# The merges of the triangular inverses: two heads in turn product by product, and the first group's second half in slot 1

## The chip, the cores and the metric

One core of a Trainium2 chip runs the whole program. The metric is the time of one execution on the device in microseconds; the time given for a kernel is the median of its runs. A profile is one further execution, recorded by the hardware profiler: its span runs from the first to the last instruction.

## What is computed

Three parts in a row: a recurrent attention over 768 steps with a 40 by 40 state for each of 32 heads, a mixture of 8 experts with one expert per token, and a dense two-layer network. The change touches the first.

```python
def _attn_ref(r, k, v, w, a, b):
    state = np.zeros((B, H, D, D))
    for t in range(S):
        y[:, :, t] = np.einsum('bhd,bhde->bhe', rt, state)
        Sa = np.einsum('bhde,bhe->bhd', state, at)
        state_decay = state * wt[:, :, None, :] - np.einsum('bhd,bhe->bhde', Sa, bt)
        state = state_decay + np.einsum('bhd,bhe->bhde', vt, kt)
    return y
```

## The kernel before

**Tiling.** The sequence is cut into chunks of 64 steps. Inside a chunk the recurrence becomes matrix products, with one triangular 64 by 64 matrix per head and chunk that has to be inverted. A *group* is 256 steps (4 chunks) of 16 heads; there are 6 groups. Heads go in pairs `u` of 8, and q = 0, 1 is the head of a pair: q=0 lies on partitions 0 to 63, q=1 on 64 to 127. A group's *half* is two of its chunks.

**Work of a group.** `prepare` (L422) loads and scales the inputs (scans on VectorE, products `abd` and `kb` on VectorE or GpSimd). `products` (L461) makes `lp` (L477), from which `l1` and `l2` are copied, and `sides` (L489) makes the transposes `bp` and `ap` (L497, L501). `inverse` (L509) is a generator with stops (`yield`). It solves the 32 by 32 diagonal blocks on VectorE with 31 pairs of instructions (L522, L524), transposes the result into `ttc` and `t11` (L530, L531), copies it into the diagonal blocks of the two tiles `tt`, one per half (L536), and then *merges*: the block of the inverse below or above the diagonal is minus the product of three 32 by 32 matrices, as `zp` (L548), a copy `z` (L550), `yp` (L554) and a negated copy into `tt` (L555). The PSUM tag "mg" has one buffer, so `zp` and `yp` alternate in one bank.

**Slots.** The 48 slots of the main loop (`run`, L675) each take one chunk of 8 heads through `sa` (L628), `tp` (L654), `rvp` (L599), `pp` (L588), `rp` (L616) and `yc` (L644). `pp`, made one slot ahead, is the first reader of `tt`; half 0 of a group is read from its first slot on, half 1 from its fifth.

**Order.** A table `plan` says in which slot and place the steps of later groups are written. With n0 the first slot of the period in which the previous group runs, `start_inverse` (L708) lets the generator make 16 steps at (n0, 0), four at (n0+2, 1) and the rest at (n0+8, 0). In the code before, those four steps end with half 0 merged, and half 1 is merged at (n0+8, 0). The first group has no slots before it: its inverse is run to its end ahead of all slots (`whole(inv)`, L743), then `first(os[1])` writes the products of group 1. Behind the first stretch, where the order is the written one, a scheduler orders the instructions of each engine by their place in the program and their readiness; each engine then works its queue in order. The two kernels below are built by it, so the order moves beyond the lines of the diff.

Of the kernel before, what the change touches and what calls it, by code (L numbers as in the profile page):

```python
# [8 lines left out]
F32 = mybir.dt.float32  # L9
# [4 lines left out]
AF = mybir.ActivationFunctionType  # L14
# [5 lines left out]
P = 128  # L20
# [211 lines left out]
def whole(gen):  # L232
    for _ in gen:
        pass
# [49 lines left out]
class Attention:  # L284
# [224 lines left out]
    def inverse(self, o):  # L509

        nc = self.nc
        l1, l2 = o.l1, o.l2
        o.tt = [self.ringed("tt", self.tt) for _ in range(2)]
        ut = self.ut0 if o.start else self.unit()
        ul = self.pa.tile([P, 32, 32], F32, name="ul", tag="t4", bufs=3)
        nc.vector.transpose(ul, l2.rearrange("p c u j -> p j (c u)"))
        yield
        for j in range(31):
            n, m = 31 - j, j + 1
            tmp = self.pa.tile([P, 256], F32, name="tmp", bufs=1)  # L520
            tv = tmp[:, :n * m].rearrange("p (a b) -> p a b", b=m)
            nc.vector.tensor_tensor(tv, ul[:, j, j + 1:].unsqueeze(2).to_broadcast([P, n, m]),  # L522
                                    ut[:, j, :m].unsqueeze(1).to_broadcast([P, n, m]), op=ALU.mult)
            nc.vector.tensor_tensor(ut[:, j + 1:, :m], ut[:, j + 1:, :m], tv, op=ALU.subtract)  # L524
            if j % 2:
                yield
        self.check(ut, ul, 0.01)
        self.check(l1.rearrange("p c u j -> p (c u) j"), ul, 0.01)
        t11, ttc = self.t4("t11"), self.t4("ttc")
        nc.vector.transpose(ttc.rearrange("p c u t -> p t (c u)"), ut)  # L530
        nc.vector.transpose(t11.rearrange("p c u s -> p s (c u)"), ut.rearrange("p t s -> p s t"))  # L531
        for half in range(2):
            for q in (1, 3, 0, 2):
                r = slice(32 * q, 32 * q + 32)
                eng = nc.vector if o.start and half == 0 else nc.gpsimd
                eng.tensor_scalar(o.tt[half][r, :, :, 32 * q:32 * q + 32], ttc[r, 2 * half:2 * half + 2], 1.0, 0.0, op0=ALU.mult, op1=ALU.add)  # L536
        yield

        for half in range(2):
            if half:  # L540
                yield
            for q in range(2):
                tt = o.tt[half]
                lo, hi = slice(q * 64, q * 64 + 32), slice(q * 64 + 32, q * 64 + 64)
                zp = self.work("zp", [P, 2, 8, 32], "mg")
                for c2 in range(2):
                    for u in range(8):
                        nc.tensor.matmul(zp[lo, c2, u], lhsT=l1[hi, 2 * half + c2, u, :], rhs=tt[hi, c2, u, q * 64 + 32:q * 64 + 64], start=True, stop=True)  # L548
                z = self.pa.tile([P, 2, 8, 32], F32, name="z1", tag="z1", bufs=1)
                nc.scalar.copy(z[lo], zp[lo])  # L550
                yp = self.work("yp", [P, 2, 8, 32], "mg")
                for c2 in range(2):
                    for u in range(8):
                        nc.tensor.matmul(yp[lo, c2, u], lhsT=t11[lo, 2 * half + c2, u, :], rhs=z[lo, c2, u, :], start=True, stop=True)  # L554
                nc.scalar.activation(tt[lo, :, :, q * 64 + 32:q * 64 + 64], yp[lo], AF.Copy, scale=-1.0)  # L555
                yield

# [115 lines left out]
    def run(self, rt, sp, moe, ctx):  # L675
        tc, nc = self.tc, self.nc
        os = []
        for bp in range(B // 2):
            for g in range(S // SL):
                o = K()  # L680
# [6 lines left out]
        def at(slot, place, fn):  # L687
            plan.setdefault((slot, place), []).append(fn)
# [25 lines left out]
        def first(o):  # L714
            self.prepare(o, 0)
            for pg in range(1, 4):
                self.prepare(o, pg)
                for c2 in range(2):
                    self.products(o, pg - 1, c2)
            for c2 in range(2):  # L720
                self.products(o, 3, c2)

        o = os[0]
# [10 lines left out]
        inv = self.inverse(o)  # L734
# [5 lines left out]
        self.count["kb"] = self.count["abd"] = 0  # L740
        with tc.issue_after(o.last_v.ins), tc.issue_after(o.last_s.ins), tc.issue_after(o.last_g.ins):
            whole(self.rest())
        whole(inv)  # L743
        self.slots_room()
        with tc.issue_after(o.last_v.ins), tc.issue_after(o.last_s.ins), tc.issue_after(o.last_g.ins):
            first(os[1])
        at(2, 0, self.empty)
# [553 lines left out]
```

## Time and profile before

| | us |
|---|---|
| median of 3 runs | 1196.84 (1193.64 to 1198.87) |
| the profiled execution | 1200.56 |
| its span | 1198.6 |
| TensorE (PE) busy in it | 1071.4 |
| VectorE (DVE) busy | 752.2 |
| ScalarE (ACT) busy | 565.2 |
| GpSimd (POOL) busy | 556.9 |

The slots begin at about 105 us and the attention ends at about 568 us; experts and dense network follow. A view by stretches gives, for each window of the span, the busy time of every engine and the mean granted clock of TensorE as a share of its full 2.4 GHz (0.50 is the lower level, 1.2 GHz). In rows of single instructions the first number is the start, the second the busy time of a run of like instructions, xN their count; starts of neighbouring rows on one engine tell what a run really took of it. "PEld" is the loading of weights.

### The profile page before, as it was taken

What the parts mean: (1) busy time and instruction counts of PE and PEld (TensorE: products, weight loads), DVE (VectorE), ACT (ScalarE), POOL (GpSimd) and SP (SyncE); (2) the same over time, 40 slices, a digit from 0 to 9 for tenths busy, and PEclk for the clock granted to TensorE, in tenths of its full rate; (3) what the DMA queues carried; (4) which work ended last, traced back from release to release, by engine and by line L of the source; (5) the groups of instructions that cost most, each with busy time, mean ns of one, the idle gap of its engine ahead of it and who ended that gap; (6) DMA issues with size and microseconds to landing.
All of it is one profiled execution on the core that took longest, in us unless ns stands there. A gap on an engine that the chain in (4) does not pass through costs nothing. (4 is left out here: it accounts for less than half of the span.)

```text
span 1198.6 us, 24763 instructions
## 1 busy us (share of the span) xinstructions
PE 1071.4 (89%) x9565; PEld 947.8 (79%) x9565; DVE 752.2 (63%) x1537; ACT 565.2 (47%) x1413; POOL 556.9 (46%) x496
## 2 busy tenths in 40 slices
PE   2579988879979899899889888999999999999997
PEld 2468767767768788677778877999899999999996
DVE  9894987867876867735369998233454444454543
ACT  3563865756765677777355434444121222121211
POOL 6663374465474452513366445445343435343433
PEclk9665987968987989988889989999999999999999
DMA  3541222222221211242569776542000000000100
GB/s 113 154 144 36 70 73 56 72 60 71 73 77 54 78 38 44 70 107 79 170 192 282 238 245 215 164 123 85 15 22 22 24 23 22 23 23 22 35 11 25
DMA packets 98080, 103.35 MB, mean 86 GB/s; under 512 B 58404, under 2 KB 78884, under 8 KB 97956
## 3 DMA queue, kind: packets, MB, share of 16 engines
q1 hardware_dynamic: 95652, 93.83, 27.1%
q0 software_dynamic: 2304, 7.87, 2.0%
q8 instruction: 78, 1.28, 0.4%
q14 instruction: 46, 0.38, 0.1%
HBM read 79.39 MB, written 22.28 MB: 85 GB/s over the span
## 5 line engine op out<-in xcount | busy, mean ns | idle before, releaser
L229 POOL TENSOR_TENSOR gl<-g,gh 128x512 fp32r<-128x512 f32 x96 | 123.9, 1294 | 211.2 <-ACT gh L228 133.0
L228 ACT ACTIVATE gh<-g 128x512 fp32r<-128x512 f32 x96 | 60.7, 632 | 249.4 <-DVE g L1193 171.5
L1192 DVE TENSOR_SCALAR g<-ph,al 128x512 f32<-128x512 f32 x96 | 72.1, 751 | 156.9 <-POOL gl L229 79.1
L238 PE MATMUL ph<-x2thi,win 128*128 128x512 f32 x480 | 157.0, 392 | 0.0
L238 PE MATMUL po<-wout,gh 128*128 128x320 f32 x768 | 139.0, 309 | 0.0
L238 PEld LDWEIGHTS po<-wout,gh 128*128 128x128 f32 x768 | 122.0, 188 | 5.4
L238 PE MATMUL ph<-x2tlo,win 128*128 128x512 f32 x288 | 113.5, 394 | 0.0
L238 PE MATMUL po<-we,hh 128*128 128x320 f32 (+1 forms) x480 | 93.1, 321 | 17.1 <-DVE hh L1068 12.9
L238 PE MATMUL ph<-xthi,we 128*128 128x448 f32 (+2 forms) x360 | 98.2, 344 | 3.3 <-DVE hl L1068 2.8
L238 PEld LDWEIGHTS ph<-x2thi,win 128*128 128x128 f32 x480 | 88.5, 188 | 13.2
L238 PEld LDWEIGHTS po<-we,hh 128*128 128x128 f32 (+1 forms) x480 | 76.1, 187 | 22.7 <-DVE hh L1068 15.3
L477 PE MATMUL lp<-kb,abd 128*128 128x128 f32 x352 | 66.4, 344 | 25.0 <-DMA tt<-in_kbP_dram 10.5
L602 POOL TENSOR_SCALAR_AFFINE_SELECT va<-vg 64x512 f32<-64x512 f32 x48 | 36.2, 755 | 107.2 <-ACT vg L601 63.6
L522 DVE TENSOR_TENSOR tmp<-ul,ut 128x31 f32<-128x31 f32 (+15 forms) x186 | 82.1, 441 | 3.4
L238 PE MATMUL po<-wout,gl 128*128 128x320 f32 x384 | 82.9, 311 | 0.0
L524 DVE TENSOR_TENSOR ut<-ut,tmp 128x31 f32<-128x31 f32 (+15 forms) x186 | 79.4, 427 | 3.4
L477 PEld LDWEIGHTS lp<-kb,abd 128*128 128x128 f32 x352 | 57.7, 246 | 29.0 <-POOL abd L458 18.3
L458 POOL TENSOR_TENSOR abd<-ra,q 40x512 f32<-40x512 f32 x44 | 62.8, 1428 | 26.5 <-PE ap L501 14.0
L238 PE MATMUL ph<-xtlo,we 128*128 128x448 f32 (+2 forms) x216 | 74.4, 346 | 0.3 <-DVE xtlo L271 0.3
L238 PEld LDWEIGHTS ph<-xthi,we 128*128 128x128 f32 x360 | 66.8, 196 | 7.3 <-issue 2.5
L644 PE MATMUL yc<-va,kbr 128*40 128x104 f32 (+3 forms) x768 | 59.7, 275 | 10.1 <-POOL abd L458 6.4
L1193 DVE SCALAR_TENSOR_TENSOR g<-ph,g 128x512 f32<-128x512 f32 x96 | 66.3, 691 | 3.1
(210 smaller groups left out, 2467.6 us busy)
## 6 DMA issues: line engine op xcount, KB each, us to landing
raw<-in_moe_w_dram SPq DMA_DIRECT2D x16, 512.0 KB
rv<-in_rvP_dram SPq DMA_DIRECT2D x48, 160.0 KB
raw<-in_moe_w_dram SPq DMA_DIRECT2D x16, 480.0 KB
kb<-in_kbP_dram SPq DMA_DIRECT2D x44, 160.0 KB
r<-in_moe_w_in_dram SPq DMA_DIRECT2D x10, 512.0 KB
r<-in_moe_w_out_dram SPq DMA_DIRECT2D x10, 512.0 KB
xs_d<-tt SPq DMA_DIRECT2D x8, 560.0 KB
raw<-in_moe_w_dram SPq DMA_DIRECT2D x16, 256.0 KB
```

The source lines that it names most:

```text
L228: nc.scalar.activation(hi, src, AF.Copy)
L229: return lo_eng.tensor_tensor(lo, src, f32(hi), op=ALU.subtract)
L238: return nc.tensor.matmul(out, lhsT=lhsT, rhs=rhs, start=start, stop=stop)
L458: nc.gpsimd.tensor_tensor(abd[r, :, q * C:(q + 1) * C], ra[r], qc[r, :, :C], op=ALU.mult)
L477: nc.tensor.matmul(lp[:, i], lhsT=abd[:, i, c2, :], rhs=kb[:, i, c2, :], start=True, stop=True)
L522: nc.vector.tensor_tensor(tv, ul[:, j, j + 1:].unsqueeze(2).to_broadcast([P, n, m]), ut[:, j, :m].unsqueeze(1).to_broadcast([P, n, m]), op ...
L524: nc.vector.tensor_tensor(ut[:, j + 1:, :m], ut[:, j + 1:, :m], tv, op=ALU.subtract)
L602: nc.gpsimd.affine_select(x.va[:C].rearrange("p a b c -> p (a b) c")[:, :, D:], x.vg[:C].rearrange("p a b c -> p (a b) c")[:, :, D:], patt ...
L644: nc.tensor.matmul(x.yc[r, i, a:], lhsT=kb[:, c], rhs=x.va[:, i, q, a:], start=True, stop=True)
L1192: nc.vector.tensor_scalar(g, ph, 0.0, al[:, f:f + 1], op0=ALU.min, op1=ALU.mult)
L1193: nc.vector.scalar_tensor_tensor(g, ph, 0.0, g, op0=ALU.max, op1=ALU.add)
```

## The change

Three things are different.

1. In a merge, the 16 products `zp` of q=0 and the 16 of q=1 are issued in turn, one of each, into one tile `zp`; likewise `yp`. Before, all four steps of q=0 came first and then those of q=1. The products, their operands and sizes are the same.
2. One tile `z` and one `zp` and `yp` serve both heads of a half. The copies remain one instruction per head, now two in a row.
3. For the first group, 17 more steps of the generator are taken ahead of the slots instead of all: half 0 is merged there, half 1 is written at (1, 1).

The generator has 20 stops instead of 22. `start_inverse` is not edited, and so its four steps at (n0+2, 1) now merge both halves of a later group, and nothing but its end is left at (n0+8, 0).

```diff
+        lows = [slice(q * 64, q * 64 + 32) for q in range(2)]
+        highs = [slice(q * 64 + 32, q * 64 + 64) for q in range(2)]
+        both = [(c2, u, q) for c2 in range(2) for u in range(8) for q in range(2)]
         for half in range(2):
             if half:
                 yield
-            for q in range(2):
-                tt = o.tt[half]
-                lo, hi = slice(q * 64, q * 64 + 32), slice(q * 64 + 32, q * 64 + 64)
-                zp = self.work("zp", [P, 2, 8, 32], "mg")
-                for c2 in range(2):
-                    for u in range(8):
-                        nc.tensor.matmul(zp[lo, c2, u], lhsT=l1[hi, 2 * half + c2, u, :], rhs=tt[hi, c2, u, q * 64 + 32:q * 64 + 64], start=True, stop=True)
-                z = self.pa.tile([P, 2, 8, 32], F32, name="z1", tag="z1", bufs=1)
+            tt = o.tt[half]
+            zp = self.work("zp", [P, 2, 8, 32], "mg")
+            for c2, u, q in both:
+                nc.tensor.matmul(zp[lows[q], c2, u], lhsT=l1[highs[q], 2 * half + c2, u, :], rhs=tt[highs[q], c2, u, highs[q]], start=True, stop=True)
+            z = self.pa.tile([P, 2, 8, 32], F32, name="z1", tag="z1", bufs=1)
+            for lo in lows:
                 nc.scalar.copy(z[lo], zp[lo])
-                yp = self.work("yp", [P, 2, 8, 32], "mg")
-                for c2 in range(2):
-                    for u in range(8):
-                        nc.tensor.matmul(yp[lo, c2, u], lhsT=t11[lo, 2 * half + c2, u, :], rhs=z[lo, c2, u, :], start=True, stop=True)
-                nc.scalar.activation(tt[lo, :, :, q * 64 + 32:q * 64 + 64], yp[lo], AF.Copy, scale=-1.0)
-                yield
+            yp = self.work("yp", [P, 2, 8, 32], "mg")
+            for c2, u, q in both:
+                nc.tensor.matmul(yp[lows[q], c2, u], lhsT=t11[lows[q], 2 * half + c2, u, :], rhs=z[lows[q], c2, u, :], start=True, stop=True)
+            for lo, hi in zip(lows, highs):
+                nc.scalar.activation(tt[lo, :, :, hi], yp[lo], AF.Copy, scale=-1.0)
+            yield
...
-        whole(inv)
+        for _ in range(17):
+            next(inv)
         self.slots_room()
+        at(1, 1, lambda: whole(inv))
```

What that does to the order, at two places. First TensorE in the start, from the first merge of the first group to the first `pp` of the slots; before (`lp`, `bp`, `ap` belong to group 1, xN counts like instructions in a row):

```order
L548 MATMUL zp<-tt_123,l_179 32x32 x16
L477 MATMUL lp<-kb_107,abd_109 128x128 x4
L497 MATMUL bp<-ident,kb_107 128x104 x4
L554 MATMUL yp<-z_561,t_532 32x32 x16
L501 MATMUL ap<-ident,abd_109 128x104 x4
L477 MATMUL lp<-kb_106,abd_108 128x128 x4
L548 MATMUL zp<-tt_123,l_179 32x32 x16
L497 MATMUL bp<-ident,kb_106 128x104 x4
L554 MATMUL yp<-z_598,t_532 32x32 x16
L501 MATMUL ap<-ident,abd_108 128x104 x4
L548 MATMUL zp<-tt_124,l_179 32x32 x16
L588 MATMUL pp<-tt_123,la 104x128 x4
```

And the same place now (line numbers of the changed code are up to three higher):

```order
L548 MATMUL zp<-tt_123,l_179 32x32 x32
L477 MATMUL lp<-kb_107,abd_109 128x128 x4
L497 MATMUL bp<-ident,kb_107 128x104 x4
L554 MATMUL yp<-z_577,t_532 32x32 x32
L501 MATMUL ap<-ident,abd_109 128x104 x4
L477 MATMUL lp<-kb_106,abd_108 128x128 x4
L589 MATMUL pp<-tt_123,la 104x128 x4
L600 MATMUL rvp<-rv_398 64x64 x8
L548 MATMUL zp<-tt_124,l_179 32x32 x26
L629 MATMUL sa<-vg_403,pw_415 64x104
```

Half 0 is two runs of 32 products now instead of four of 16, and half 1 (`tt_124`), one `bp` and one `ap` stand behind the first `pp`.

Second, TensorE at the boundary to group 1, ahead of the first `pp` of slot 8, which reads half 0 (`tt2_125`); before:

```order
L497 MATMUL bp_1980<-ident_60,kb1_107 128x104 x4
L501 MATMUL ap_1986<-ident_60,abd1_109 128x104 x4
L554 MATMUL yp_1352<-z1_1350,t11_1284 32x32 x16
L477 MATMUL lp_1999<-kb1_107,abd1_109 128x128 x4
L497 MATMUL bp_2009<-ident_60,kb1_107 128x104 x4
L588 MATMUL pp_1940<-tt2_125,la_732 104x128 x4
```

And now:

```order
L554 MATMUL yp_1326<-z1_1323,t11_1278 32x32 x32
L497 MATMUL bp_2042<-ident_60,kb1_107 128x104 x4
L501 MATMUL ap_2048<-ident_60,abd1_109 128x104 x4
L548 MATMUL zp_1361<-tt0_123,l1_653 32x32 x32
L589 MATMUL pp_2002<-tt2_125,la_655 104x128 x4
```

The second head's `yp` has gone into the first one's run, and `zp` of half 1 (`tt0_123`) has come ahead of `pp`.

## Rows read from the trace of the kernel before

**Rows 1.** The page: busy time of the engines, and PEclk in 40 slices.

```profile
PE 1071.4 (89%) x9565; PEld 947.8 (79%) x9565; DVE 752.2 (63%) x1537; ACT 565.2 (47%) x1413; POOL 556.9 (46%) x496
...
PEclk9665987968987989988889989999999999999999
```

**Rows 2.** Busy time by stretch: length, PE, PEld, DVE, ACT, POOL, clock, DMA.

```profile
89.00:115.00 26.00, 25.60 (x285) 22.97 (x286) 9.94 (x19) 8.26 (x21) 11.54 (x15) 0.50 0.09 27
115.00:172.00 57.00, 49.78 (x690) 41.55 (x689) 51.81 (x119) 41.53 (x130) 27.37 (x30) 0.94 0.27 68
172.00:213.00 41.00, 35.47 (x490) 31.13 (x490) 28.91 (x71) 23.02 (x70) 20.87 (x21) 0.79 0.22 60
213.00:250.00 37.00, 29.30 (x372) 24.85 (x369) 35.66 (x78) 25.03 (x79) 21.04 (x21) 0.91 0.31 82
250.00:304.00 54.00, 49.79 (x653) 42.18 (x653) 32.61 (x85) 33.30 (x102) 26.89 (x30) 0.78 0.22 57
304.00:350.00 46.00, 38.56 (x511) 32.45 (x509) 42.77 (x107) 33.77 (x109) 28.00 (x31) 0.96 0.31 80
350.00:400.00 50.00, 47.53 (x619) 41.62 (x619) 34.22 (x81) 28.62 (x85) 24.37 (x27) 0.76 0.21 59
400.00:430.00 30.00, 25.00 (x279) 21.07 (x278) 27.95 (x67) 20.44 (x66) 17.48 (x17) 0.83 0.22 59
430.00:468.00 38.00, 37.10 (x637) 32.16 (x633) 23.02 (x69) 29.01 (x87) 14.65 (x22) 1.00 0.19 46
468.00:500.00 32.00, 28.27 (x423) 22.80 (x424) 28.83 (x88) 24.31 (x73) 10.75 (x14) 1.00 0.26 60
500.00:530.00 30.00, 26.71 (x471) 23.18 (x468) 9.76 (x34) 19.22 (x55) 9.70 (x15) 0.89 0.23 58
```

**Rows 3.** Timeline of the start (start, length, engine, line, operation, tiles), clock 0.50.

```profile
88.14 3.48 DVE L536 TENSOR_SCALAR tt<-ttc 32x512 f32<-32x512 f32 x4
...
89.40 1.91 PE L548 MATMUL zp<-tt,l 32*32 32x32 f32 x32 [0.80 <-DVE tt L536]
...
103.87 1.91 PE L548 MATMUL zp<-tt,l 32*32 32x32 f32 x32
105.71 2.04 PE L588 MATMUL pp<-tt,la 128*104 128x128 f32 x8
107.68 1.12 PE L599 MATMUL rvp<-rv 64*64 64x64 f32 x16
108.73 1.91 PE L554 MATMUL yp<-z,t 32*32 32x32 f32 x32
```

**Rows 4.** Timeline of TensorE at full clock, in slots 0 and 2.

```profile
115.69 1.19 PE L548 MATMUL zp<-tt,l 32*32 32x32 f32 x32
116.82 0.68 PE L616 MATMUL rp<-rv,bds 64*64 64x64 f32 x16
...
126.61 0.68 PE L599 MATMUL rvp<-rv 64*64 64x64 f32 x16
127.22 1.12 PE L588 MATMUL pp<-tt,la 128*104 128x128 f32 x8
128.27 0.39 PE L644 MATMUL yc<-va,kbr 128*64 128x104 f32 x2
```

**Rows 5.** Groups of TensorE instructions from 85 to 560 us: count, busy, idle before.

```profile
L554 PE MATMUL yp<-z,t 32*32 32x32 f32 x768 | 35.2, 208 | 2.2 <-ACT z L550 1.7 <-DVE t L531 0.5
L548 PE MATMUL zp<-tt,l 32*32 32x32 f32 x768 | 34.6, 203 | 1.5 <-DVE tt L536 0.8 <-POOL tt L536 0.7
```

**Rows 6.** Timeline at the boundary to group 1, two copies and slot 8's first product.

```profile
174.09 0.59 ACT L555 ACTIVATE tt<-yp 32x512 f32<-32x512 f32 x1
...
181.16 0.58 ACT L555 ACTIVATE tt<-yp 32x512 f32<-32x512 f32 x1
...
181.79 1.12 PE L588 MATMUL pp<-tt,la 128*104 128x128 f32 x8
```

## Prediction

> **What bounds the kernel now.** I began with the page: TensorE (PE) is busy for 1071.4 of 1198.6 us, but its granted clock (PEclk) moves between full and half level all through the attention part and is nearly steady after it [rows 1]. The change touches the attention part alone, so I cut that part into stretches and read the busy time of every engine in each [rows 2]. Two kinds of stretch take turns. In 115-172, 213-250, 304-350, 400-430 and 468-500 us VectorE (DVE) is full, 187.0 of 202 us: there the solve of the next group runs. In 89-115, 172-213, 250-304, 350-400, 430-468 and 500-530 us PE is full, 222.2 of 239 us, with DVE at 138.5 us: there lie the merges, `zp` and `yp`. So PE time that a merge gives up is time in the stretches where PE ends last, and what follows them (the next solve, later the mixture of experts) starts when they end. Rows of single instructions then price a block of products [rows 3, 4].
>
> **Part 1, two heads product by product.** Each merge product is 32 by 32 and leaves two records; 16 products of one head make a block of 32 records. The trace has 768 + 768 records, so 48 blocks, with 34.6 + 35.2 = 69.8 us of PE [rows 5]. Blocks come in two sizes: from one start to the next instruction's start 1.84 us at half clock (103.87 to 105.71, clock 0.50) and 1.13 us at full clock (115.69 to 116.82) [rows 2, 3, 4]. With busy times of 1.91 and 1.19 us, 69.8 us makes about 18 blocks at half and 30 at full clock (48 x 1.19 = 57.1; the other 12.7 divided by 0.72).
>
> In the code before, all 32 records of a block use the same 32 rows and 32 columns of the array. Now q=0 and q=1 alternate, on other rows and other columns. No row shows that for 32 by 32. The nearest is `rvp`: its 16 records of 64 by 64 alternate between two halves of rows and columns. They take 0.61 us at full clock (126.61 to 127.22) and 1.05 at half (107.68 to 108.73) [rows 3, 4]. Products that use the whole width, `pp` with 128 columns, take 1.05/8 = 0.131 and 1.97/8 = 0.246 us a record [rows 3, 4]; half of that for 64 columns, times 16, is 1.05 and 1.97 us. So alternating cost 0.58 (full) and 0.53 (half) of the time in turn: two tiles run side by side. For two blocks as one of 64 records I take the same shares: 2 x 1.13 x 0.58 = 1.31 us (0.95 saved) and 2 x 1.84 x 0.53 = 1.95 us (1.73 saved). Over 24 pairs, 15 at full and 9 at half clock, PE gives up 14.3 + 15.6 = 30 us. Bounds: nothing, if small tiles don't overlap, and 34 us, half of 69.8 rounded down.
>
> One rule speaks against this, and the rows speak against the rule. `rvp` writes both its halves into one PSUM tile of 1 KB per partition, alternately, and still costs 0.58 of the price in turn [rows 4]. The Trainium skill (TensorEngine Tiling (Array Packing), Gotcha 1: PSUM Pressure) says that different row tiles cannot access the same PSUM bank simultaneously; by it the 30 us would be nothing and rival 1 below would hold. The skill's TensorE: Matmul & The Clock Gate (Part 1, Wait — 56ns, not 53.3ns?) gives about 25 ns as the least distance of two starts; as an estimate 64 records would then take 1.6 us instead of 1.31 at full clock, and the gain would be about 3 us smaller. No row of this case goes below it.
>
> **Part 2, copies.** The code still issues one `z` copy and one negated copy into `tt` per head, so ScalarE (ACT) does the same 48 instructions; "shared" means that two stand in a row in one tile. That removes round trips PE to ACT to PE: a half needs two instead of four. At the boundary to group 1 the second head's round trip runs from the end of `tt` at 174.68 to the end of the next at 181.74, 7.1 us, and the `pp` of slot 8 follows at 181.79 [rows 6]. In the order, `pp` now stands behind one `yp` and the next half's `zp`. I don't add these 7 us to the sum: PE was full there with other work, which has to be done all the same. It is the reason why the PE time that is saved reaches `pp` at all. The price: one more `tt` copy (0.59 us [rows 6]) ahead of what stands behind it on ACT.
>
> **Part 3, the first group's half 1 behind the first slot.** In the start PE works without a gap at clock 0.50, 25.60 of 26 us [rows 2]. The chain goes from `zp` at 89.40 to the first `pp` at 105.71 [rows 3]. Of five blocks ahead of `pp`, four remain, as two pairs, and one `bp` and `ap` move behind it. Moved work comes back a few us later on the same full engine, so only the pairs count: three at half and one at full clock, 3 x 1.73 + 0.95 = 6.1 us. The added wait: product 2 of the first `zp` needs the second of the four DVE copies that take 3.48 us from 88.14 [rows 3], one copy later, up to 0.9 us; `lp`, `bp` and `yp` queue behind it on PE and nothing covers it. Start: -6.1 + 0.9, about -5 us. What is late next is DVE: it did 9.94 us in those 26 [rows 2], waiting for slot 0, and then has 57 full us, which begin as much earlier.
>
> **Part 4, the other groups' half 1.** The generator now stops less often, so the four steps at slot n0+2 run half 1 too; before it ran at n0+8. In the order, `zp` of half 1 stands ahead of the new group's first `pp`, and its `yp` ahead of the first `sa`: up to 1.31 us each, on the path of that slot. They cover the two `tt` copies (1.18 us), and slots 8 and 9 lose four blocks. I count this as nothing; without the overlap of part 1 it costs 2 x 2.26 us at full clock.
>
> **Sum.** Outside the start 30 - 6 = 24 us of PE go. The ends are 24, if PE stays the last in all these stretches, and a third of that, if DVE, ACT and POOL chains take over. PE already stood idle for 17 of 239 us there, and DVE and ACT are loaded to 60% [rows 2]; I take 60%, 14.5 us, nearer the upper end since PE was at 93%. Start 5 + boundaries 14.5, about 20 us. The MoE part shifts as a whole, since its loads begin at a slot of the last group, behind the last merge. The profiled execution: 1200.56 us (span 1198.6) - 20 = 1180.6. It lies 3.7 us above the median of the runs, 1196.84; against the median the forecast is **1177 us**. About 0.5% (6 us) is what a measurement of this kernel can tell from no change.
>
> **Rivals.**
> 1. *Small tiles don't overlap.* The products still take turns on PE, the order changes, the work doesn't. For it: no row shows 32 by 32 tiles alternating. Against it: `rvp` in both clocks. What stays is one `bp` and `ap` out of the way in the start and fewer round trips, which were mostly filled: -3 us, 1194. Chance 0.10.
> 2. *Another engine takes over at once.* DVE has 30 to 35 us of work in the 50 us stretches, and each slot is a chain through PE, ACT, DVE and POOL. If only a third of the 30 us arrives, start included: -9 us, 1188. For it: 87% in 172-213, with waits of PE; against it: 92 to 98% in four of the six. Chance 0.17.
> 3. *Slower: the clock falls.* The five later merge stretches (213 us) had a mean clock of 0.83 [rows 2]. With fewer records in the same slots PE waits more often, and behind the stretches in which it idled most (7.7 us in 213-250, 7.4 in 304-350) the clock was 0.78 and 0.76, behind 5.0 and 3.7 us 1.00 and 0.89. PE work of 213 - 24 = 189 us at 0.83 takes 189 x 0.83/c at clock c. It decides below c = 0.72, where that is 219 us and eats the start's gain too; at 0.68 it is 231: +18 - 6, 1209. For it: that sequence; against it: the merge stretches themselves stay dense, since `lp`, `bp` and `ap` fill them. Chance 0.10.
> 4. *The forecast*, 1177. Chance 0.63.
>
> **How the numbers follow.** The likeliest case gives 1177. The range must leave out no more than 2 in 10: its low end is 34 us saved in all, 1164 (0.05 below); its high end takes in rivals 1 and 2, to 1196 (0.13 above, most of it rival 3). Faster by over 0.5% is the forecast with 0.63 and three quarters of rival 2, 0.76; within 0.5% is rival 1 and the rest of 2, 0.14; slower is rival 3, 0.10.
>
> **What will show it.** A `zp` or `yp` of 64 records should take about 1.3 us at full and 2.0 us at half clock, and all merges together about 40 us instead of 69.8; near 2.4 and 3.7 says rival 1. The first `pp` should start near 100 us. The first `sa` of slots 8, 16, 24, 32 and 40 should come 8, 11, 14, 17 and 20 us earlier in turn. If merges shrink and these don't, PE's idle time or PEclk in the merge stretches says whether rival 2 or 3 took it. A loss that begins only behind the attention part would make all of this wrong.

## The result, and the profile after

The changed kernel takes 1180.3 us (median of four runs, 1179.85 to 1183.18); the kernel before, run beside it, 1197.9 us. The ratio is 0.986, with a 95% interval of 0.983 to 0.990. Run once more beside the second set of experiments, it gave 0.984 (0.980 to 0.988). The forecast was 1177, from 1164 to 1196. The one profile of the kernel before is of a slower run (1200.56 us) than its four timed ones, so the two profiles differ by 20.7 us where the medians differ by 17.6.

The page of the profiled execution (1179.85 us, span 1178.0), the lines that answer to [rows 1]: TensorE is busy for 40.7 us less, ScalarE and GpSimd are where they were.

```profile
PE 1030.7 (87%) x9565; PEld 908.3 (77%) x9565; DVE 746.1 (63%) x1537; ACT 565.3 (48%) x1413; POOL 557.2 (47%) x496
...
PEclk9668979978889999789989999999999999999999
```

The groups of TensorE instructions from 85 to 560 us that answer to [rows 5] (count, busy us, mean ns, then idle time before them and what ended it): as many records as before, in 37.6 us instead of 69.8. In front of them PE now waits for 13.3 us instead of 3.7.

```profile
L548 PE MATMUL zp<-tt,l 32*32 32x32 f32 x768 | 20.4, 214 | 9.2 <-ACT tt L556 2.6 <-POOL yt L665 2.4 <-POOL kb L454 1.7
L554 PE MATMUL yp<-z,t 32*32 32x32 f32 x768 | 17.2, 198 | 4.1 <-issue 2.8 <-ACT z L551 1.3
```

Two views of the whole attention part, from 88 us to the last `sa`, first of the kernel before, then of the changed one (stretch, length, busy time of PE, PEld, DVE, ACT, POOL, granted clock, DMA share, GB/s). PE lost 37.9 us and the stretch became 19 us shorter, so PE's time without work grew from 53.0 to 71.8 us. DVE has the same work in less time.

```profile
88.00:566.00 478.00, 425.03 (x5848) 361.52 (x5847) 347.94 (x870) 318.09 (x954) 225.46 (x253) 0.86 0.25 66
```

```profile
88.00:547.00 459.00, 387.17 (x5860) 325.19 (x5861) 344.91 (x871) 318.38 (x953) 226.94 (x254) 0.89 0.27 68
```

The same view cut as in [rows 2], at the points where the changed kernel's merges begin and end. Merges lie in 89-105, 160-198, 246-285, 331-372, 409-437 and 474-515 us, the solve of the next group between them.

```profile
89.00:105.00 16.00, 14.75 (x284) 12.99 (x282) 10.91 (x16) 7.98 (x21) 12.09 (x14) 0.74 0.14 43
105.00:160.00 55.00, 46.34 (x651) 38.94 (x651) 50.62 (x122) 39.64 (x125) 24.35 (x24) 0.91 0.26 64
160.00:198.00 38.00, 32.40 (x556) 27.64 (x554) 24.15 (x58) 26.17 (x78) 24.43 (x28) 0.91 0.27 74
...
246.00:285.00 39.00, 33.77 (x543) 29.01 (x544) 25.07 (x58) 25.31 (x76) 22.90 (x26) 0.82 0.24 66
...
331.00:372.00 41.00, 33.07 (x541) 28.33 (x541) 25.73 (x58) 23.45 (x67) 23.73 (x27) 0.83 0.22 58
...
409.00:437.00 28.00, 27.31 (x551) 23.70 (x549) 15.25 (x34) 25.78 (x74) 13.05 (x21) 0.96 0.23 58
437.00:474.00 37.00, 33.35 (x506) 27.21 (x505) 34.98 (x117) 28.13 (x88) 11.35 (x14) 1.00 0.24 53
474.00:515.00 41.00, 27.30 (x492) 23.34 (x494) 18.95 (x45) 27.10 (x65) 11.14 (x16) 0.73 0.40 108
```

Before, PE was busy for 93% of the merge stretches; now it is 92, 85, 87, 81, 98 and 67% in the six. The last row is the one that has no counterpart before: in 500 to 530 us the clock was 0.89 and PE was busy for 26.71 of 30 us [rows 2].

The first `sa` of a slot, from the two timelines, shows how the gain builds up and where some of it goes:

| slot | 0 | 8 | 16 | 24 | 32 | 39 | 40 | 42 | 47 | end of span |
|---|---|---|---|---|---|---|---|---|---|---|
| before | 110.6 | 185.5 | 278.0 | 369.8 | 449.4 | 500.9 | 515.8 | 531.0 | 564.1 | 1198.6 |
| after | 101.9 | 180.6 | 265.9 | 351.7 | 428.5 | 473.9 | 494.0 | 515.3 | 545.6 | 1178.0 |
| earlier by | 8.7 | 4.9 | 12.1 | 18.1 | 20.9 | 27.0 | 21.8 | 15.7 | 18.5 | 20.6 |

It is 27 us at slot 39, and 11 of them are lost again by slot 42. A second profile of the changed kernel (the second set below) repeats it: 26 us at slot 39 (474.5) and 16 at slot 42 (514.6).

### The profile page after: what moved, and what is told of

It is laid out like the page before. It is cut to its first block, busy times and chain, and to the rows that moved or that the text cites. A ratio compares the mean times of both kernels' runs of the same rounds, so it can differ in the third digit from the quotient of the medians.

```text
span 1178.0 us, 24786 instructions
## 1 busy us (share of the span) xinstructions
PE 1030.7 (87%) x9565; PEld 908.3 (77%) x9565; DVE 746.1 (63%) x1537; ACT 565.3 (48%) x1413; POOL 557.2 (47%) x496
## 5 line engine op out<-in xcount | busy, mean ns | idle before, releaser
L238 PEld LDWEIGHTS ph<-x2thi,win 128*128 128x128 f32 x480 | 88.7, 188 | 13.1
L477 PE MATMUL lp<-kb,abd 128*128 128x128 f32 x352 | 62.1, 330 | 24.6 <-DVE s L455 10.6
L522 DVE TENSOR_TENSOR tmp<-ul,ut 128x31 f32<-128x31 f32 (+15 forms) x186 | 78.9, 424 | 3.4
L458 POOL TENSOR_TENSOR abd<-ra,q 40x512 f32<-40x512 f32 x44 | 61.9, 1408 | 33.7 <-issue 12.1
L477 PEld LDWEIGHTS lp<-kb,abd 128*128 128x128 f32 x352 | 53.6, 232 | 28.6 <-POOL abd L458 19.1
L589 PE MATMUL pp<-tt,la 128*104 128x128 f32 x384 | 63.1, 315 | 5.1 <-DVE lg L889 5.1
```

What stands on the lines that cost most here:

```text
L238: return nc.tensor.matmul(out, lhsT=lhsT, rhs=rhs, start=start, stop=stop)
L458: nc.gpsimd.tensor_tensor(abd[r, :, q * C:(q + 1) * C], ra[r], qc[r, :, :C], op=ALU.mult)
L477: nc.tensor.matmul(lp[:, i], lhsT=abd[:, i, c2, :], rhs=kb[:, i, c2, :], start=True, stop=True)
L589: nc.tensor.matmul(pp[:, i], lhsT=o.la[x.half][:, x.c2, u, :], rhs=o.tt[x.half][:, x.c2, u, :], start=True, stop=True)
```

## The experiments

Three questions stood after the result: is it the overlap of the two tiles that pays, or the fewer round trips; what are the two moves of second halves worth; and what takes 11 us at the last boundary? My theory was that the overlap brings about all of it, that the moves are small, and that the last boundary loses by two waits. The rivals stand with each run. Runs of one kernel spread over 3 to 22 us, so a single profile shows a mechanism and the medians of several runs show a price. "The base" below is a kernel of the third set.

### First set: the parts one by one

**The pairing alone.** The changed kernel, but the generator stops and the start run as before:

```
-            at(n0 + 2, 1, lambda: [next(inv) for _ in range(4)])
+            at(n0 + 2, 1, lambda: [next(inv) for _ in range(3)])
...
-        for _ in range(17):
-            next(inv)
+        whole(inv)
         self.slots_room()
-        at(1, 1, lambda: whole(inv))
```

> The two heads' products take turns as in the changed kernel, but the first group's second half is merged before the slots, and the later groups' second halves at slot n0+8, as in the kernel before. Theory (the pair of 32x32 tiles costs TensorE what one tile cost, and the two moved halves are separate and small): TensorE busy time falls by 38 to 42 us as in the changed kernel, to about 1030 us; a run of 64 zp or yp records takes about 1.2 us at the full clock and 1.9 us at half; the first sa of slot 2 comes about 4 us earlier than before instead of 10; the time is 1184 to 1187 us, a ratio of about 0.989 to the kernel before. Rival 1 (most of the gain is the first group's half that moved behind slot 1): the time is 1191 us or more. Rival 2 (merging the second half early is what gave time back at the last boundary): the boundary at slots 39 to 41 gives nothing back, and the time is 1180 us or less although the start is longer.

Measured: 1175.4 us, ratio 0.984 (0.975 to 0.993); PE busy 1030.5 us; slot 2's `sa` at 117.1 instead of 124.1. Without the two moves the time is no worse than the whole change's. My theory had 1184 to 1187 us, because it took the moves for a gain. The attention part ends early (last slot's `sa` at 534.2 against 545.6), as rival 2 said, but some of that does not reach the end; see the late halves below.

**The first group's half alone.** The kernel before with only this part:

```
-        whole(inv)
+        for _ in range(18):
+            next(inv)
         self.slots_room()
+        at(1, 1, lambda: whole(inv))
```

> The kernel before, with one head merged after the other as there; only the first group's second half is merged in slot 1 instead of ahead of the slots. Theory (the start is a matter of its own): slot 0's first sa comes 5 to 6 us earlier, half of that comes back when the half is merged in slot 1, and the time is about 1192 to 1194 us, a ratio near 0.996; TensorE's busy time stays at 1071 us within 3. Rival (what stands ahead of the slots only moves, since slot 2 needs that half): the time is that of the kernel before within 2 us.

Measured: 1199.2 us, ratio 1.002 (0.997 to 1.007), PE busy 1065.9 us. No gain, and the rival holds: slot 0 came 1.6 us earlier (109.0 against 110.6) and slot 2 2.2 us (121.9 against 124.1), and nothing of that is left in the time.

**One head, then the other.** One line of the changed kernel:

```
-        both = [(c2, u, q) for c2 in range(2) for u in range(8) for q in range(2)]
+        both = [(c2, u, q) for q in range(2) for c2 in range(2) for u in range(8)]
```

> The changed kernel with one edit: the 16 products of one head, then the 16 of the other, as the kernel before has them within a head; the two heads still share a PSUM tile, and the round trips from TensorE to ScalarE and back stay at two for each half. Theory (the tiles of two heads overlap when they stand next to each other): a run of 64 takes 2.4 us at the full clock and 3.8 us at half, TensorE's busy time is back within 5 us of 1071, and 10 to 18 us of the 18 come back: 1190 to 1198 us. Rival (the gain comes from two round trips instead of four): the time stays within 4 us of the changed kernel's 1180 us although TensorE is busy for 40 us more. In between, the shares can be read: what stands above 1180 is the overlap, what is left below 1198 is the trips and the start.

Measured: 1185.0 us, ratio 0.994 (0.990 to 0.998); PE busy 1048.8 us, so 18 us came back and not 40. The merges took 57.5 us in this profile, against 69.8 before and 37.6 in the changed kernel; a run of 64 took less than the 2.4 and 3.8 us that were expected. The time lies between the rival's 1184 and the theory's 1190. Timelines of PE: first this kernel, a run at half and one at full clock, then the changed kernel, one at full and one at half.

```profile
99.11 3.43 PE L554 MATMUL yp<-z,t 32*32 32x32 f32 x64
...
167.51 2.11 PE L548 MATMUL zp<-tt,l 32*32 32x32 f32 x64
```

```profile
108.10 1.20 PE L554 MATMUL yp<-z,t 32*32 32x32 f32 x64
...
487.93 1.92 PE L548 MATMUL zp<-tt,l 32*32 32x32 f32 x64 [2.65 <-ACT tt L556]
```

Same records, same tile, same copies; only the turn differs, and it is 1.20 against 2.11 us and 1.92 against 3.43 us. That is the overlap, seen directly. The time says the same with less sharpness. Read as expected, 1185 less 1180 us, the overlap would be worth only 5 us; but beside this set the kernel before took 1194.6 us and not 1197.9, so the ratios are what can be compared: 0.994 against 0.984 to 0.986, so the larger part of the gain hangs on the turns. What is left, 0.994, is the shared round trips, the moves and what the scheduler made of them.

**The later halves at their old place.** The first of the two edits of the pairing alone, range(3), without the second.

> The changed kernel with one number back: a later group's second half is merged at slot n0+8 as before, not at n0+2. Theory of the prediction (that move costs nothing): 1180 us within 3, and the slots 39 to 41 still give back about 9 us of the 25 that had been won by slot 34. Rival (with no other TensorE work left at the last boundary, the second half's two products stand ahead of slot 40's products and copies and hold them up): slot 39 takes 15 to 16 us instead of 20, and the time is 1172 to 1176 us. A third outcome, slower than 1183 us, would mean that the early merge earns something at the inner boundaries.

Measured: 1171.3 us, ratio 0.982 (0.975 to 0.989). In this set alone that can't be told from 0.986, but the profile shows what the move does. Timelines of PE at the boundary to group 3: the changed kernel, then the late halves.

```profile
336.63 0.88 PE L554 MATMUL yp<-z,t 32*32 32x32 f32 x43
...
342.76 1.92 PE L548 MATMUL zp<-tt,l 32*32 32x32 f32 x64
344.61 2.04 PE L589 MATMUL pp<-tt,la 128*104 128x128 f32 x8
346.58 1.11 PE L617 MATMUL rp<-rv,bds 64*64 64x64 f32 x16
347.62 2.08 PE L477 MATMUL lp<-kb,abd 128*128 128x128 f32 x8
349.49 0.67 PE L497 MATMUL bp<-ident,kb 104*128 104x104 f32 x4
350.09 1.20 PE L554 MATMUL yp<-z,t 32*32 32x32 f32 x64
351.22 0.58 PE L501 MATMUL ap<-ident,abd 104*128 104x104 f32 x4
351.73 0.93 PE L629 MATMUL sa<-vg,pw 128*64 128x104 f32 x16
```

```profile
336.21 1.20 PE L554 MATMUL yp<-z,t 32*32 32x32 f32 x64
...
339.40 1.12 PE L589 MATMUL pp<-tt,la 128*104 128x128 f32 x8
...
342.47 0.44 PE L548 MATMUL zp<-tt,l 32*32 32x32 f32 x16
342.84 0.39 PE L629 MATMUL sa<-vg,pw 128*64 128x104 f32 x2
```

The new group's first slot needs only half 0. In the changed kernel half 1's `zp` stands ahead of `pp` and its `yp` ahead of `sa`, and while the copies between the two run, PE goes on with the next group's `lp` and `bp`: from the first `zp` record of half 0 to the new group's first `sa` it is 20.9 us (330.8 to 351.7) against 12.7 us (330.1 to 342.8). Part of that is the clock: in the changed kernel it was at half from 339.6 to 349.8 us, with the late halves it was full all through. In the second profile of the changed kernel, where it was full here too, the distance is 14.7 us. Over the five boundaries these distances add up to 99.7 us before, 92.3 after (86.9 in the second profile) and 71.4 with the late halves (71.8 to 75.3 in the three profiles of the later sets that have them). So the boundaries, which the pairing could have made 28 us shorter in all, became 7 to 13 us shorter.

At the last boundary the view by stretch over slots 39 to 42 (kernel before, changed, late halves) gives 37.7, 47.4 and 35.6 us:

```profile
500.90:538.60 37.70, 32.35 (x543) 27.46 (x541) 15.52 (x43) 26.30 (x71) 11.21 (x17) 0.91 0.39 100
```

```profile
473.90:521.30 47.40, 33.70 (x578) 28.52 (x574) 20.94 (x51) 31.27 (x78) 12.47 (x18) 0.75 0.37 98
```

```profile
472.40:508.00 35.60, 28.98 (x515) 24.19 (x511) 18.28 (x48) 28.25 (x73) 10.36 (x15) 0.86 0.50 123
```

PE is busy for about as long as before and idle for 13.7 us instead of 5.4 (6.6 with the late halves); the clock fell with it. Slot 39 takes 20.1 us in the changed kernel and 10.0 with the late halves, less than the rival's 15 to 16. With it the solve ends later against the slots: its `ttc` transpose starts at 475.82, 1.9 us behind slot 39's first `sa`; with the late halves at 467.54, 4.9 us ahead of it, so that slot 39's own work lies beside the merge. What makes the solve late, DVE being full before it (34.98 of 37 us in 437 to 474) or the order of its steps, I did not separate.

The late halves' last `sa` is 14.6 us earlier than the changed kernel's, but the profiled span only 6.6 us shorter (1171.4 against 1178.0). Timeline of PE behind the last slot, changed kernel and late halves:

```profile
546.84 1.15 PE L238 MATMUL xp<-xw,yt 128*128 128x112 f32 x8
...
549.23 0.66 PE L265 MATMUL tr_ps<-ident,raw 128*128 128x128 f32 x4
```

```profile
532.39 1.12 PE L238 MATMUL xp<-xw,yt 128*128 128x112 f32 x8
...
538.09 1.11 PE L265 MATMUL tr_ps<-ident,raw 128*128 128x128 f32 x4 [3.21 <-DMA raw<-xs_d]
```

The first expert's rows are scattered by GpSimd and read back by a DMA before they are transposed. With less attention left behind the router, PE stands for 3.2 us in front of that load, the clock falls to half for 10 us from 537.5 on, and the first expert product (`ph`) comes 8.2 us earlier than in the changed kernel instead of 14.6. The load is issued at 535.0 us, 3 us behind the last `sa`; in the changed kernel at 546.2, just ahead of it (546.7). That this is no fixed bound shows below, where both edits are made.

### Second set: the last boundary

**The changed kernel again**, as the yardstick.

> The changed kernel once more, beside the next three, so that they are compared with it on the same chip: a ratio of 0.986 to the kernel before, within 0.004.

Measured: 1174.1 us, 0.984 (0.980 to 0.988).

**The weights held to their slots.** In slots 40 and 41 of the changed kernel ScalarE's timeline reads:

```profile
502.88 1.00 ACT L1021 ACTIVATE we<-raw 128x960 fp32r<-128x960 f32 x1 [0.38 <-DMA raw<-in_moe_w_dram]
505.28 1.00 ACT L1021 ACTIVATE we<-raw 128x960 fp32r<-128x960 f32 x1 [1.40 <-DMA raw<-in_moe_w_dram]
506.31 0.66 ACT L613 COPY vg<-sm 40x160 f32<-40x160 f32 x2
506.99 0.43 ACT L888 COPY xr<-xp 128x320 f32<-128x320 f32 x1
508.75 0.74 ACT L1021 ACTIVATE we<-raw 128x640 fp32r<-128x640 f32 x1 [1.33 <-DMA raw<-in_moe_w_dram]
509.39 0.41 ACT L888 COPY xr<-xp 128x320 f32<-128x320 f32 x1
```

and PE's, in the same place, 5.4 us of waiting for DVE's `lg`, which stands behind the same weights on DVE:

```profile
507.69 1.12 PE L600 MATMUL rvp<-rv 64*64 64x64 f32 x16 [3.69 <-DVE lg L889]
...
510.50 2.04 PE L589 MATMUL pp<-tt,la 128*104 128x128 f32 x8 [1.69 <-DVE lg L889]
```

DVE before the second of these waits:

```profile
509.51 0.82 DVE L1022 TENSOR_TENSOR we<-raw,we 128x640 fp32r<-128x640 f32 x1 [1.88 <-ACT we L1021]
510.25 0.18 DVE L889 TENSOR_REDUCE lg<-xp 128x8 f32<-128x32 f32 x1
```

These pieces (`we`) are written in the program for slots 43 to 45. In the kernel before they ran at 531.5 to 546.5 us, from slot 42 on; the scheduler took them forward when the change moved the rest. The edit, with the copy in `stage_a` kept as `self.sa_i`:

```
+            def held():
+                with tc.issue_after(self.sa_i.ins):
+                    next(pre)
+
             for m in range(6):
-                at(n_slots - 5 + m // 2, 2, lambda: next(pre))
+                at(n_slots - 5 + m // 2, 2, held)
```

> The changed kernel with one edit: each of the six pieces of the first expert's weight preparation is queued on ScalarE behind the copies of the sa tile of its own slot (43 to 45), so that the scheduler can no longer put them into slots 40 and 41 ahead of the router's copies. Theory A (in the changed kernel ScalarE stood for 3.1 us in front of these pieces for their loads, with the router's and slot 42's copies behind it): slot 41 falls from 13.5 to 6 to 8 us, and the time by 3 to 6 us, to a ratio of about 0.982. Theory B (slot 41 is long because the clock is at half there, and the pieces fill time in which ScalarE would wait anyway): slot 41 stays above 11 us and the time does not move by more than 2 us, or rises, since the same pieces then stand in slots 43 to 45 where nothing is waited for.

Measured: 1169.1 us, 0.980 (0.976 to 0.984), against the changed kernel's 0.984 beside it. Slot 41 took 5 us instead of 13.1. The profile agrees with theory A; the time moved by 4 to 5 us, which the two intervals don't separate, and a second run of this kernel (third set) gave 0.983. Of the 8 us in slot 41, 5 come back in slots 43 to 46, where the pieces now stand: from slot 42 to the last `sa` it is 33.8 us against 28.8. So this is worth 0 to 5 us.

**Both edits.**

> The changed kernel with both edits: later groups' second halves at slot n0+8, and the weight pieces held to their slots. Theory (each edit takes away one of the two waits of the last boundary, and what stands behind attention, the router's rows and their load, takes most of the second gain back): last sa 2 to 5 us earlier than with the late halves alone (531 us), but a time within 3 us of that kernel's 1171 us. Rival (nothing behind attention holds it): the whole 2 to 5 us show in the time, 1166 to 1169 us.

Measured: 1167.3 us, 0.980 (0.975 to 0.984); the last `sa` stood at 527.6 us in the profile. The median lies in the rival's range and just below the theory's; the late halves with more fillers, the next run of this set, took 1170.1, and the intervals don't separate the two. In the profile the tail is not what the theory said. The load behind the router is issued at 526.1 us, ahead of the last `sa`, and PE does not wait for it. From the last `sa` to the end it is 632 us, as in the changed kernel (631), where the late halves alone have 639. In the third set's run of the same kernel it is 629.

**More filler products.** The late halves, and

```
-            if 40 <= n < 48:
+            if 36 <= n < 48:
```

> The changed kernel with later groups' second halves at slot n0+8, and with the four filler products of each of the slots 40 to 47 also in slots 36 to 39: 16 products of 128x128 more, which nothing reads. It measures what the clock's falls at the last boundary cost. Theory A (the two falls to half clock there, 3.4 and 6.8 us long with the late halves, cost about half their length): the granted clock stays at full from 460 to 510 us and the time falls by 3 to 5 us. Theory B (what is slow there waits for copies, and not for TensorE): the clock rises but the time stays within 2 us of the kernel without these fillers, or is 1 us longer for the 16 products.

Measured: 1170.1 us, 0.979 (0.975 to 0.983): no difference from the late halves. It settles nothing on the clock. The fillers wait for nothing, and the scheduler had put all of them, the old ones too, into slots 33 to 35, where the clock was full anyway. The tile's instructions, with the late halves alone and with more fillers (count, least, median and longest in ns, first and last start):

```profile
L238 PE MATMUL warm<-ones x32: 219/219/230, 431.6 to 440.8; 128*128 128x128 bf16 x32
```

```profile
L238 PE MATMUL warm<-ones x48: 216/219/230, 432.2 to 445.2; 128*128 128x128 bf16 x48
```

The falls came all the same, 10.2 us long from 452.3 and from 496.7 on. What the clock costs at the last boundary stays open.

### Third set: prices with everything else equal

All four kernels hold the weight pieces, so that the scheduler can't move them; the first is the base.

> The changed kernel with the first expert's weight pieces held behind the sa copies of slots 43 to 45, once more: the base of the next three, all with the pieces held, so that the last boundary's wait for loads is out of the comparison. A ratio to the kernel before of 0.980 within 0.004.

Measured: 1175.0 us (1173.2 to 1177.4), 0.983 (0.978 to 0.988).

> As the base, with the 16 products of one head and then those of the other. It measures what the overlap of the two heads' tiles is worth with everything else equal. Theory (about half of the TensorE time saved shows in the time, as it did for the whole change: TensorE busy time 18 us up, as without the held pieces): 8 to 10 us slower than the base, a ratio of 0.987 to 0.989. Rival (what is saved inside a run of products is waited for behind it, since the copies of the two heads come one after the other in both): 3 us or less.

Measured: 1186.3 us, 0.997 (0.993 to 1.001), 11 us slower than the base with 24 us more of PE time. The overlap is worth that much; the rest of the change, shared round trips and both moves taken together, brings nothing that can be measured here.

> As the base, but with the first group's second half ahead of the slots and the later groups' second halves at slot n0+8, as in the kernel before: the pairing alone, with the pieces held. Theory of the prediction (moving the first group's half is worth about 5 us, moving the later halves nothing): 4 to 6 us slower than the base. Rival (the two moves only shift work between slots): within 2 us of the base. If it is over 3 us faster, the moves cost time.

Measured: 1166.8 us (1161.3 to 1175.5), 0.976 (0.970 to 0.981): 8 us faster than the base. Neither the theory nor the rival; the third case holds, and the two moves together cost time.

> As the base, but with the later groups' second halves at slot n0+8: the price of that move alone. Theory of the prediction: within 2 us of the base. Rival (it costs time at the last boundary): 3 us or more faster than the base, as the one profiled run of this kernel was, whose last sa stood 13 us earlier.

Measured: 1167.0 us (1164.5 to 1173.5), 0.978 (0.972 to 0.983): 8 us faster than the base, as fast as without the first group's move. The intervals overlap by a little, but in either kernel five of the six runs are faster than every run of the base. So it is the later halves' move that costs, and the first group's that is worth nothing. With the second set, where the same pair of kernels stood 2 us apart, the price is 2 to 8 us.

Both of the last kernels beat the changed one: 1167 against 1174 to 1180 us, at ratios of 0.976 to 0.980.

## Why the prediction came out right, point by point

The time was 1180.3 where 1177 was forecast, and the profiled execution 1179.85 where 1180.6 was. The main term was right. That the total came out so close was luck in part, since errors went against each other. The pairing without the two moves was worth 1.6%, and 2.4% with the weight pieces held (19 and 29 us), where the sum had about 20 for boundaries and start together; and the later halves' move, counted at nothing, cost 2 to 8 us. The first group's move gave nothing that can be measured.

**Part 1** held, and was sized a little low. The shares from `rvp`, 0.58 and 0.53, were on the safe side. From its start to the next instruction's a pair takes 1.13 us at full clock (350.09 to 351.22) and 1.85 at half (342.76 to 344.61) instead of the forecast 1.31 and 1.95, a share of 0.50; that is what one block of one head took before, 1.13 and 1.84 [rows 3, 4]. The merges fell to 37.6 us where about 40 was forecast, 32 us saved where I said 30. PE's whole busy time fell by 40.7; the remaining 8 us were not in the sum. Between 5 and 6 of them lie in the attention part and go with its mean clock of 0.89 instead of 0.86, at which the other products are shorter too. The rule on PSUM that spoke against the overlap (the Trainium skill, TensorEngine Tiling (Array Packing), Gotcha 1: PSUM Pressure) doesn't describe these tiles: both heads write into one PSUM tile, and 64 records take the time of 32. Nor did the 25 ns between two starts (the Trainium skill, TensorE: Matmul & The Clock Gate, Part 1, Wait — 56ns, not 53.3ns?) bind here: 1.20 us for 64 records is 18.8 ns each. That no row went below it holds for the means alone: in the trace of the kernel before, 374 of the 768 records of `rvp` start 4 to 7 ns behind the record ahead of them.

**Part 2** was left out of the sum, and no run shows it alone. With shared round trips but no overlap the ratio was 0.994 and 0.997; but those two kernels also have the later halves' move, which costs 2 to 8 us, and the round trips may have paid for it.

**Part 3** holds in what it says of the start; its -5 us can't be told apart in the time. They are the saving of pairs, so taking the move away does not test them. The pairing alone brings the first `sa` of slot 0 forward by 3.1 us (107.5 against 110.6) and that of slot 2 by 7.0 (117.1 against 124.1). With the move on top slot 0 comes another 1.4 and 1.9 us earlier (106.1 against 107.5 in the first set, 105.0 against 106.9 in the third), and the time shows nothing of it (1167.0 against 1166.8 us with and without it). Without the pairing the move's gain is gone by slot 8 (185.6 against 185.5), and its ratio is 1.002.

The first `pp` started at 99.26 where "near 100" was forecast. That this fits so well is luck in part: the first `zp` started 1.8 us later than before, behind DVE's copies, and from 97.2 us on the clock was full, which the forecast did not have. In the second profile, at half clock throughout, the chain from the first `zp` to the first `pp` takes 9.6 us (93.43 to 103.07), against 8.1 here and 16.3 before, so it did become shorter by about what was forecast. Timeline of DVE and PE in the start, answering to [rows 3]:

```profile
89.92 3.48 DVE L536 TENSOR_SCALAR tt<-ttc 32x512 f32<-32x512 f32 x4
```

```profile
91.19 0.31 PE L548 MATMUL zp<-tt,l 32*32 32x32 f32 x2 [0.80 <-DVE tt L536]
91.95 1.91 PE L548 MATMUL zp<-tt,l 32*32 32x32 f32 x62 [0.45 <-DVE tt L536]
...
96.49 1.48 PE L554 MATMUL yp<-z,t 32*32 32x32 f32 x64
99.26 1.12 PE L589 MATMUL pp<-tt,la 128*104 128x128 f32 x8
```

The added wait was forecast at up to 0.9 us, and its row shows 0.45.

**Part 4** failed: "I count this as nothing". I priced it as two runs of 1.31 us that cover two copies. The rows at the boundary to group 3 show 1.92 us at half clock, and the copy between `zp` and `yp`, and the `lp` and `bp` that PE took up while it waited for it, all ahead of the first `sa`. At the boundary to group 1, where `pp` stood at 181.79 [rows 6], it came 7.8 us earlier, at 173.95, but the `sa` behind it only 4.9 us, at 180.56.

**The share of 60%** was somewhat high. Of 38 us that PE lost in the attention part, 19 arrived, half of them, by the two profiles. DVE takes over where I said, full for 34.98 of 37 us ahead of the last boundary, and a part of rival 2 is thus in the result. With the late halves more arrives in the attention part; the 8 us that this kernel loses again behind it, at the router's scatter and load, are not lost where the weight pieces are held as well.

**The mixture of experts** was to shift as a whole, "since its loads begin at a slot of the last group, behind the last merge". Its preparation did not shift: the scheduler took it into slots 40 and 41, ahead of its loads. From the first `sa` of slot 39 on the gain fell by 11 us, of which the second halves and these weights are the two causes found.

**The slots.** Forecast for 8, 16, 24, 32 and 40: 8, 11, 14, 17 and 20 us; measured: 4.9, 12.1, 18.1, 20.9 and 21.8. Rival 3 came true in one stretch: the clock fell in the last merges, from 0.89 to 0.73, hardly in the fifth, from 1.00 to 0.96, and rose in the other four.

## What to carry to other kernels

When small products of two independent heads lie in different rows and columns of the array, let them take turns one by one, and look at the length of the run in the timeline: it is that of one head. Before merging such work earlier, ask whether the next consumer needs it; what it doesn't need should stand behind that consumer in PE's order, however short it is. And after each change compare where a scheduler put work that was not touched: an instruction that waits for a load on an in-order engine costs more than it does.

## What the runs showed that I had not expected

- Two 32 by 32 tiles in turn cost what one costs, at both levels of the clock: 1.20 and 1.92 us for 64 records, against 2.11 and 3.43 us with the heads one after the other. `rvp`'s 64 by 64 tiles had come to 0.58 and 0.53 of the price in turn, not to half [rows 3, 4].
- Filler products that depend on nothing don't stay where the program has them. With the late halves the 32 written for slots 40 to 47 ran from 431.6 to 440.8 us, in slots 33 and 34, and with 16 more the last ran at 445.2, some 7 us ahead of the next fall of the clock.
- What stands behind the attention can take back what was won in it, and need not. With the late halves alone it is 5.7 us from the start of the last slot's first `xp` to the first transpose (532.39 to 538.09), against 2.4 us in the changed kernel (546.84 to 549.23). With the weight pieces held as well, the attention ends as early (last `sa` at 527.6 and 533.9 us), and it is 2.2 and 2.8 us: the load of the scattered rows is then issued ahead of the last `sa`. The pairing alone shows the same difference, 638 us from the last `sa` to the end without the pieces held and 630 with them; why was not looked into.
